# K's first head in one transfer and inside the loop, wo in six transfers, ten semaphores fewer

## The chip, the cores and the metric

The kernel runs on one core of one Trainium2 chip. The metric is the device time of one execution in microseconds. Before the change the median of three runs is 1363.03 us (1362.77 to 1363.04).

## What is computed

One decode step for one token: a layer norm, then attention over a cache of 16384 keys for 32 heads of 128, and beside it a gated feed-forward block; both are added to the input. All data is float32. Cut to what matters:

```python
# x (1,1,576); k_cache, v_cache (1,32,16384,128); wq (576,4096); wo (4096,576)
# w_gate, w_up (576,4608); w_down (4608,576)
xn = layernorm(x)
q = (xn @ wq).reshape(32, 128)
scores = einsum("hd,hkd->hk", q, k_cache) * 128 ** -0.5
a = einsum("hk,hkd->hd", softmax(scores), v_cache).reshape(4096) @ wo
g, u = xn @ w_gate, xn @ w_up
return x + a + (gelu(g) * u) @ w_down
```

The two caches are 537 MB of the 588 MB that are read.

## The kernel before

Every large operand passes through three buffers of 64 KB on each of 128 partitions: slot_a, slot_b and slot_v (sa, sb and sv in the code). One head of K or of V fills one of them whole (8.389 MB).

SP issues all large loads, in the order of its program, and each waits on SP until its buffer is free; so the order in the code is the order in the queue. First wq (sa) and the parts of wq, w_gate and w_up that go elsewhere, then w_gate's main part (sb), w_up's (sa), K's first head in two halves (sb, L380 to L382), K's second head (sa), V's first (sv). Then a loop (L387) alternates K and V: K's next head goes out when VectorE has given back a K slot (semaphore s_kf), V's next when TensorE has given back sv (s_vf). Behind the loop come 28 rows of w_down (sb), V's last head (sv), the rest of w_down (sa), and wo: its first 8 rows of each partition into sa, the other 24 into sb, over rows of w_down that VectorE has already summed.

VectorE computes the scores. For a head it multiplies the K slot by q (qs, broadcast), reduces over 128 elements, then takes the maximum over each partition (pm); TensorE transposes pm, and VectorE reduces that to nm. K's first head is done in front of the loop in two parts of 64 rows (L427 to L433), then 15 turns of two heads each (L434), then the last head (L437). ScalarE turns the scores into exponentials (pe, L450) and makes the next q; TensorE multiplies pe with V (L405). TensorE's loop runs 32 times, ScalarE's five loops together 32 times.

In front of that, x comes by three small loads that ScalarE issues: once as a row (xrow, for the layer norm) and once cut in two (x2, to be added at the end). The identity matrix ident is made by GpSimd; VectorE reduces it to small selection matrices (par, same, quarter, sel_p, sel_r, sel_l).

Behind the loops VectorE sums 28 rows of w_down, each times its element of h (L467 to L469), and 20 pieces of its last half row; TensorE takes the rest of w_down and the 32 rows of wo from the slots. wo's last twelve rows go in quarters to four PSUM banks (pg, pqs, po, pc), its very last row comes in two half rows; four copies and one DMA write the output.

Class Order records for each written region which semaphore value says that it is done, and sets the waits from that. A plain `load` makes a semaphore of its own (d0, d1, ...). `take(engine, s, n)` waits for n and subtracts it again.

Of the kernel before, what the change touches and what calls it, by code (L numbers as in the profile page):

```python
# [10 lines left out]
ALU = mybir.AluOpType  # L11
AX = mybir.AxisListType

P = 128
H, SK, DH = 32, 16384, 128
D, DF = 576, 4608
R = SK // P
SUB = 64
DJ = 4
DM = P * DJ  # L20
SCALE = DH**-0.5
# [1 line left out]
HALF = D // 2  # L23
# [3 lines left out]
WD_T = DF // P  # L27
# [1 line left out]
FB = (11 * WD_T, 11 * WD_T, 10 * WD_T)  # L29
WO_T = HD // P  # L30
WD_A = 28
WO_PIECES = (8, 12, 4, 4, 2, 1, 1)
WO_A = 8
WO_Q = 12
QUART = D // 4
FEW, EACH, RUN = 5, 4, 6
MANY, GROUP = FEW * EACH, EACH * RUN + 1
LEFT = P - FEW * EACH * RUN
# [5 lines left out]
class Order:  # L44
# [3 lines left out]

    def __init__(self, tc):
        self.tc, self.nc = tc, tc.nc  # L50
        self.sem = {e: tc.alloc_semaphore(f"s_{e}") for e in self.ENGINES[1:]}
        self.count = dict.fromkeys(self.sem, 0)
        self.seen = {e: {} for e in self.ENGINES}
        self.log = {}
# [36 lines left out]
    def op(self, eng, emit, out, *ins, also=(), signal=None, quiet=False):  # L91
        reads, writes = [a for a in ins if a is not None], [out, *also]
        need = self.needs(eng, reads, writes)
        for sem, value in need[:-1]:
            getattr(self.nc, eng).wait_ge(sem, value)
        i = emit(getattr(self.nc, eng))
        if need:
            i._wait_ge(*need[-1])
        value = self.count[eng] + 1
        if quiet:  # L100
            pass
        elif signal is None:
            self.count[eng] = value
            i.then_inc(self.sem[eng], 1)
        else:
            i.then_inc(signal, 1)
        self.note(eng, self.sem[eng], value, reads, writes)

    def dma(self, dst, src, sem, value=16, eng="sync", out=False):
        need = self.needs(eng, [src] if out else [], [] if out else [dst])  # L110
# [49 lines left out]
def decode(tc, x, k_cache, v_cache, wq, wo, wg, wu, wd, out, slots, s_ends):  # L160
# [5 lines left out]
    def sem():  # L166
        return tc.alloc_semaphore(f"d{next(names)}")
# [50 lines left out]
    def dve(name, out, *ins, **kw):  # L218
        o.op("vector", lambda e: getattr(e, name)(out, *ins, **kw), out, *[a for a in ins if isinstance(a, bass.AP)],  # L219
             *[a for a in kw.values() if isinstance(a, bass.AP)])  # L220
# [4 lines left out]

    spent = []

    def load(dst, src, again=False, **kw):
        if again and spent:
            o.dma(dst, src, spent.pop(0), value=32, **kw)  # L230
        else:
            s = sem()
            o.dma(dst, src, s, **kw)
            if kw.get("eng") != "scalar":
                spent.append(s)
        return dst

    ROW3 = 3 * DF
# [1 line left out]
    qt = load(sb[:, ROW3 : ROW3 + QS], wtail["q"])  # L240
    row3, tails, at = {}, {}, 0
    for n in "gu":
        row3[n] = load(sv[:, at : at + DF], wmain[n][:, ROW3:])
        tails[n] = load(sv[:, at + DF : at + DF + DF // 2], wtail[n])
        at += DF + DF // 2

    xrow = sv[:1, ROW3 + FG : ROW3 + FG + D]
    load(xrow, xf, eng="scalar")
    o.op("gpsimd", lambda e: e.memset(x2, 0.0), x2)
    s_x = sem()  # L250
    for i in range(2):
        o.dma(x2[32 * i : 32 * i + 1, :], xf[:, i * HALF : (i + 1) * HALF], s_x, value=32, eng="scalar")
    o.op("gpsimd", lambda e: e.memset(ident, 0.0), ident)
    o.op("gpsimd", lambda e: e.affine_select(out=ident, in_=ident, compare_op=ALU.not_equal, fill=1.0, base=0,
                                             pattern=[[-1, P]], channel_multiplier=1), ident, ident)
    o.op("vector", lambda e: e.memset(ones, 1.0), ones)
    o.op("vector", lambda e: e.memset(eps_t, EPS), eps_t)
    s_ap, s_vp, s_pa, s_v, s_pt, s_vf, s_kf, s_qf, s_qd, s_d, s_a = (tc.alloc_semaphore(f"h{n}") for n in range(11))
    s_k = [tc.alloc_semaphore(f"k{n}") for n in range(2)]
    for bank, s in ((PO, s_pa), (pc, None), (pq, None)):  # L260
        o.op("vector", lambda e, bank=bank: e.memset(bank, 0.0), bank, signal=s)
# [91 lines left out]
            i = nc.tensor.matmul(dst, lhs, rhs, start=start, stop=stop)  # L353
        i.then_inc(s, 1)

    def take(e, s, n=1):
        e.wait_ge(s, n).then_inc(s, -n)  # L357

    def head(h):
        return bass.ds(h, 1)  # L360
# [13 lines left out]
    def load_k(h, dst, s):  # L374
        nc.sync.dma_start(dst, kv[:, head(h), :].rearrange("p h f -> p (h f)")).then_inc(s_k[s], 16)

    def load_v(h):
        nc.sync.dma_start(sv, vv[:, head(h), :].rearrange("p h f -> p (h f)")).then_inc(s_v, 16)

    parts = [(sb[:, i * SUB * DH : (i + 1) * SUB * DH], S[:, i * SUB : (i + 1) * SUB]) for i in range(R // SUB)]  # L380
    for i, (dst, _) in enumerate(parts):
        load(dst, kv[:, 0, i * SUB * DH : (i + 1) * SUB * DH])  # L382
    o.wait("sync", [], [sa])
    load_k(1, sa, 1)
    o.wait("sync", [], [sv])
# [1 line left out]
    with nc.sync.Fori(0, (H - 2) // 2) as i:  # L387
        for s, dst in ((0, sb), (1, sa)):
            take(nc.sync, s_kf)
            load_k(i * 2 + (2 + s), dst, s)  # L390
            take(nc.sync, s_vf)
            load_v(i * 2 + (1 + s))

    with nc.Fori(0, H, engines=OrderedEngineSet([KIND["tensor"]]), head_slot={KIND["tensor"]: 0}):
        take(nc.tensor, s_ap)
# [12 lines left out]

    def highest(sc):
        nc.vector.reduce_max(pm, sc, axis=AX.X).then_inc(s_vp, 1)  # L410
        take(nc.vector, s_pt)
        nc.vector.tensor_reduce(nm[:1], pt[:1, :P], axis=AX.X, op=ALU.max, negate=True).then_inc(s_vp, 1)  # L412

    def scores_of(kt, s):
        sc = S[:, s * R : s * R + R]
        blk = kt.rearrange("p (n d) -> p n d", d=DH)
        take(nc.vector, s_k[s], 16)
        take(nc.vector, s_qd)
        nc.vector.tensor_mul(blk, blk, qs.unsqueeze(1).to_broadcast([P, R, DH])).then_inc(s_d, 1)  # L419
        nc.vector.wait_ge(s_d, 1).then_inc(s_qf, 1)  # L420
        nc.vector.tensor_reduce(sc, blk, axis=AX.X, op=ALU.add).then_inc(s_d, 1)  # L421
        nc.vector.wait_ge(s_d, 2).then_inc(s_kf, 1)
        take(nc.vector, s_d, 2)
        highest(sc)

    take(nc.vector, s_qd)
    for src, sc in parts:  # L427
        blk = src.rearrange("p (n d) -> p n d", d=DH)
        dve("tensor_mul", blk, blk, qs.unsqueeze(1).to_broadcast([P, SUB, DH]))
        dve("tensor_reduce", sc, blk, axis=AX.X, op=ALU.add)  # L430
    nc.vector.wait_ge(o.sem["vector"], o.count["vector"]).then_inc(s_kf, 1)
    nc.vector.nop().then_inc(s_qf, 1)
    highest(S[:, :R])  # L433
    with nc.vector.Fori(0, (H - 2) // 2):  # L434
        scores_of(sa, 1)
        scores_of(sb, 0)
    scores_of(sa, 1)  # L437

    for h0, n in ((0, 6), (6, 8), (14, 8), (22, 8), (30, 2)):
        row, lo = divmod(min(h0 + 2, H - 1), H // 4)  # L440
        with nc.scalar.Fori(0, n) as i:
            take(nc.scalar, s_pa)
            nc.scalar.activation(z, PO, AF.Copy).then_inc(s_ap, 1)  # L443
            take(nc.scalar, s_pa)
            take(nc.scalar, s_qf)
            nc.scalar.activation(qs, pq[:, :DH], AF.Copy).then_inc(s_qd, 1)
            take(nc.scalar, s_pa)
            nc.scalar.activation(nb, pb[:, :1], AF.Copy, scale=SCALE).then_inc(s_a, 1)  # L448
            take(nc.scalar, s_a)
            nc.scalar.activation(pe, S[:, bass.ds(i % 2 * R, R)], AF.Exp, bias=nb, scale=SCALE, accum_out=lsum[:, bass.ds(i + h0, 1)]).then_inc(s_ap, 1)  # L450
            take(nc.scalar, s_pa)
            nc.scalar.activation(oall[:, bass.ds(i + h0, 1)], pc[:, :1], AF.Copy)
            src = q_part(min(h0 + 2, H - 1)) if n == 2 else qb[32 * row : 32 * row + 1, bass.ds(i * DH + lo * DH, DH)]
            nc.scalar.activation(qcur, src, AF.Copy).then_inc(s_ap, 1)

    def load_rows(t, at, src, lo, n, cols=((0, D),)):
        for a, b in cols:
            if b - a == D:
                load(t[:, at * D : (at + n) * D], src[:, lo * D : (lo + n) * D], again=True)
            else:  # L460
                load(t[:, at * D + a : at * D + b], src[:, lo * D + a : lo * D + b], again=True)
        return [t[:, (at + j) * D : (at + j + 1) * D] for j in range(n)]

    take(nc.sync, s_kf)
# [6 lines left out]
    load_v(H - 1)  # L471
    take(nc.sync, s_kf)
    n = (WD_T - WD_A) * D - HALF
    load(sa[:, :n], wdv[:, WD_A * D : WD_T * D - HALF], again=True)
    wd_rows = [sa[:, j * D : (j + 1) * D] for j in range(WD_T - WD_A)]
    few = sa[AT : AT + MANY, n : n + (RUN + 1) * HALF]
    s_few, src = sem(), wdv[:, WD_T * D - HALF :]
    by_q = src[: FEW * GROUP].rearrange("(q t) f -> q t f", q=FEW)
    o.dma(few[:, : RUN * HALF], by_q[:, : GROUP - 1, :], s_few, value=48)
    o.dma(few[:FEW, RUN * HALF :], by_q[:, GROUP - 1, :], s_few, value=48)  # L480
    o.dma(few[FEW:LEFT, RUN * HALF :], src[FEW * GROUP :], s_few, value=48)
    few_sum = few[:, :HALF]
    dve("tensor_scalar", few_sum, few_sum, few_h[many, :1], None, op0=ALU.mult)
    for r in range(1, RUN + 1):
# [104 lines left out]
```

## Time and profile before

| what | us |
|---|---|
| median of three runs | 1363.03 |
| lowest and highest | 1362.77, 1363.04 |
| the profiled execution | 1362.84 |
| its span in the trace | 1361.1 |

| engine | busy us | share of the span |
|---|---|---|
| PE (TensorE matmul) | 445.6 | 33% |
| DVE (VectorE) | 1163.2 | 85% |
| ACT (ScalarE) | 68.6 | 5% |
| POOL (GpSimd) | 1.0 | 0% |

The span is the time between the first and the last event of the execution in the trace; times of rows count from its start. DMA engines do not stand in this table: the profile gives their mean busy share by slice, with the GB/s that they moved. SPq and ACTq are the sequencers of SP and ScalarE, which issue DMAs. "To landing" is the time from an issue to the arrival of its last byte.

### The profile page before, as it was taken

How to read it: one execution, taken by the hardware profiler on the slowest of the kernel's cores; microseconds unless marked ns; L12 is line 12 of the kernel's file. 1: busy time of each engine (PE TensorE's matmuls, PEld its weight loads, DVE VectorE, ACT ScalarE, POOL GpSimd, SP SyncE). 2: the span in 40 equal slices, each digit the busy share in tenths (PEclk: the TensorE clock that was granted, in tenths of full speed). 3: DMA queues.
4: the chain of work that ended last, by engine and by line, in shares of the span. 5: the costliest groups of instructions: out<-in, count | busy, mean ns of one | idle time of the engine just before them, and what ended most of it. 6: DMA issues, size and time to landing. Idle time of an engine off the chain costs nothing. (4 is left out here: it accounts for less than half of the span.)

```text
span 1361.1 us, 7835 instructions
## 1 busy us (share of the span) xinstructions
PE 445.6 (33%) x3032; PEld 162.0 (12%) x3032; DVE 1163.2 (85%) x208; ACT 68.6 (5%) x238; POOL 1.0 (0%) x7
## 2 busy tenths in 40 slices
PE   2431233323322333323223333233223333332236
PEld 1110111101111111101111111011111111011012
DVE  1069999999888888898888888998888889988883
ACT  0000000000000000000000000000000000000000
POOL 0000000000000000000000000000000000000000
PEclk9775666666556666666556666655566666655668
DMA  9999999999999999999999999999999999999998
GB/s 403 445 424 431 443 441 435 431 431 431 435 431 433 431 431 443 441 435 431 431 431 435 431 433 431 431 443 439 435 433 431 431 435 431 433 431 431 442 442 354
DMA packets 12106, 587.69 MB, mean 432 GB/s; under 512 B 1345, under 2 KB 1731, under 8 KB 1989
## 3 DMA queue, kind: packets, MB, share of 16 engines
q1 hardware_dynamic: 12093, 587.60, 99.7%
q8 instruction: 5, 0.08, 0.0%
q10 hardware_dynamic: 8, 0.01, 0.0%
HBM read 587.60 MB, written 0.00 MB: 432 GB/s over the span
## 5 line engine op out<-in xcount | busy, mean ns | idle before, releaser
L353 PE MATMUL po<-slot_v,pe 128*4 128x512 f32 x2048 | 291.5, 733 | 578.4 <-PEq L357 578.4
L419 DVE TENSOR_TENSOR slot_a<-slot_a,qs 128x16384 f32<-128x16384 f32 x16 | 275.6, 17226 | 34.9 <-DVEq L357 34.8
L419 DVE TENSOR_TENSOR slot_b<-slot_b,qs 128x16384 f32<-128x16384 f32 x15 | 258.4, 17226 | 32.3 <-DVEq L357 32.2
L421 DVE TENSOR_REDUCE scores<-slot_a 128x128 f32<-128x16384 f32 x16 | 275.5, 17220 | 2.3
L421 DVE TENSOR_REDUCE scores<-slot_b 128x128 f32<-128x16384 f32 x15 | 258.3, 17220 | 2.2
L353 PEld LDWEIGHTS po<-slot_v,pe 128*4 128x4 f32 x2048 | 56.4, 98 | 786.5 <-issue 786.5
L398 PE MATMUL pg<-ident,pm 128*1 128x128 f32 x32 | 11.9, 372 | 239.9 <-PEq L357 239.9
L443 ACT ACTIVATE z<-po 128x512 f32<-128x512 f32 x32 | 19.1, 597 | 827.8 <-ACTq L357 827.8
L353 PE MATMUL pc<-same,z 128*128 128x1 f32 x256 | 59.8, 355 | 0.0
L353 PEld LDWEIGHTS pc<-same,z 128*128 128x128 f32 x256 | 57.1, 328 | 0.5
L219 DVE TENSOR_TENSOR slot_v<-pg,same 128x396 f32<-128x396 f32 (+1 forms) x6 | 3.3, 558 | 52.2 <-PE pg L216 52.0
L398 PEld LDWEIGHTS pg<-ident,pm 128*1 128x1 f32 x32 | 2.5, 79 | 245.2 <-issue 245.2
L412 DVE TENSOR_REDUCE nm<-pg 1x1 f32<-1x128 f32 x32 | 8.9, 278 | 21.5 <-DVEq L357 21.5
L353 PE MATMUL pg<-nm,ones 1*128 1x1 f32 x64 | 17.7, 343 | 18.5 <-PEq L357 18.5
L219 DVE SCALAR_TENSOR_TENSOR slot_b<-slot_b,hT 128x576 f32<-128x576 f32 x27 | 22.1, 819 | 0.9
L353 PE MATMUL pqs<-qcur,ones 1*128 1x128 f32 x64 | 14.8, 312 | 21.9 <-PEq L357 20.7
L353 PEld LDWEIGHTS pg<-nm,ones 1*128 1x128 f32 x64 | 15.9, 308 | 27.8 <-issue 27.8
L448 ACT ACTIVATE nb<-pg 128x1 f32<-128x1 f32 x32 | 5.5, 172 | 243.1 <-ACTq L357 243.1
L219 DVE TENSOR_REDUCE scores<-slot_b 128x64 f32<-128x8192 f32 x2 | 17.4, 8686 | 0.1
L219 DVE TENSOR_TENSOR slot_b<-slot_b,qs 128x8192 f32<-128x8192 f32 x2 | 17.4, 8688 | 0.0
L410 DVE TENSOR_REDUCE pm<-scores 128x1 f32<-128x128 f32 x32 | 9.2, 286 | 8.2 <-DVEq L357 7.9
L353 PEld LDWEIGHTS pqs<-qcur,ones 1*128 1x128 f32 x64 | 9.6, 187 | 49.9 <-issue 49.9
(109 smaller groups left out, 158.2 us busy)
## 6 DMA issues: line engine op xcount, KB each, us to landing
slot_b<-in_A_k_cache_dram SPq DMA_DIRECT2D x2, 4096.0 KB, 24.1
slot_b<-in_B_w_down_dram SPq DMA_DIRECT2D x1, 8064.0 KB, 42.0
slot_b<-in_B_w_gate_dram SPq DMA_DIRECT2D x1, 6912.0 KB, 55.1
slot_a<-in_B_w_up_dram SPq DMA_DIRECT2D x1, 6912.0 KB, 37.9
slot_b<-in_A_wo_dram SPq DMA_DIRECT2D x1, 3456.0 KB, 27.6
slot_v<-in_B_w_gate_dram SPq DMA_DIRECT2D x1, 2304.0 KB, 28.7
slot_v<-in_B_w_up_dram SPq DMA_DIRECT2D x1, 2304.0 KB, 37.1
slot_a<-in_A_wo_dram SPq DMA_DIRECT2D x1, 2304.0 KB, 31.1
```

The lines of the kernel that those rows point to most:

```text
L219: o.op("vector", lambda e: getattr(e, name)(out, *ins, **kw), out, *[a for a in ins if isinstance(a, bass.AP)], *[a for a in kw.values() i ...
L353: i = nc.tensor.matmul(dst, lhs, rhs, start=start, stop=stop)
L398: nc.tensor.transpose(pt[:1, :P], pm, ident).then_inc(s_pt, 1)
L410: nc.vector.reduce_max(pm, sc, axis=AX.X).then_inc(s_vp, 1)
L412: nc.vector.tensor_reduce(nm[:1], pt[:1, :P], axis=AX.X, op=ALU.max, negate=True).then_inc(s_vp, 1)
L419: nc.vector.tensor_mul(blk, blk, qs.unsqueeze(1).to_broadcast([P, R, DH])).then_inc(s_d, 1)
L421: nc.vector.tensor_reduce(sc, blk, axis=AX.X, op=ALU.add).then_inc(s_d, 1)
L443: nc.scalar.activation(z, PO, AF.Copy).then_inc(s_ap, 1)
L448: nc.scalar.activation(nb, pb[:, :1], AF.Copy, scale=SCALE).then_inc(s_a, 1)
```

## The change

K's first head is loaded whole with load_k, as every other head is, and VectorE's loop runs 16 turns from the first head to the last; the code in front of it and behind it goes. In the SP queue one transfer of 8.389 MB stands where two halves stood:

```order
L113 DMA slot_a<-in_B_w_up_dram 128x13824 [waits s_tensor]
L113 DMA slot_b<-in_A_k_cache_dram 128x8192 [waits d7,s_tensor]
L113 DMA slot_b<-in_A_k_cache_dram 128x8192 [waits d0,s_tensor]
L375 DMA slot_a<-in_A_k_cache_dram 128x16384 [waits s_tensor,d8]
L378 DMA slot_v<-in_A_v_cache_dram 128x16384 [waits d4,d3,s_vector,d2,d1]
```

That was SP before its loop in the kernel before; and this is the same place in the changed kernel:

```order
L115 DMA slot_a<-in_B_w_up_dram 128x13824 [waits s_tensor]
L378 DMA slot_b<-in_A_k_cache_dram 128x16384 [waits s_tensor,d4,d0]
L378 DMA slot_a<-in_A_k_cache_dram 128x16384 [waits s_tensor,d5]
L381 DMA slot_v<-in_A_v_cache_dram 128x16384 [waits s_vector,d2,d1]
L389 UNCONDITIONAL_BRANCH
```

The whole head waits for w_gate's main part (now d4) and for q's tail (d0), for which the two halves waited one each. On VectorE, from the last step of the feed-forward block to the loop, before (h8 says that qs is there, h4 that TensorE has transposed pm):

```order
L219 TENSOR_TENSOR slot_b<-slot_b,qs 128x8192 [waits h8,d7,d9]
L219 TENSOR_REDUCE scores<-slot_b 128x64 [waits s_vector]
L219 TENSOR_TENSOR slot_b<-slot_b,qs 128x8192 [waits d10]
L219 TENSOR_REDUCE scores<-slot_b 128x64 [waits s_vector]
L410 TENSOR_REDUCE pm<-scores 128x1 [waits s_vector]
L412 TENSOR_REDUCE nm<-pg 1x1 [waits h4]
L434 UNCONDITIONAL_BRANCH
L419 TENSOR_TENSOR slot_a<-slot_a,qs 128x16384 [waits k1,h8]
```

and now (h7 says that qs is there, k0 and k1 that the K slots are filled):

```order
L430 UNCONDITIONAL_BRANCH
L423 TENSOR_TENSOR slot_b<-slot_b,qs 128x16384 [waits k0,h7]
L425 TENSOR_REDUCE scores<-slot_b 128x128 [waits s_vector]
L414 TENSOR_REDUCE pm<-scores 128x1 [waits s_vector]
L416 TENSOR_REDUCE nm<-pg 1x1 [waits s_tensor]
L423 TENSOR_TENSOR slot_a<-slot_a,qs 128x16384 [waits k1,h7]
```

The multiply starts with the whole head in its slot, and the loop begins with slot_b. In the same loops three semaphores give way to the engines' own, with their count at that point as the base (a_base, pt_base, d_base).

wo comes in pieces of 16, 8, 4, 3 and 1 rows (the last in two halves) instead of 8, 12, 4, 4, 2, 1 and 1; 16 rows go to slot_a instead of 8. SP's last transfers before:

```order
L113 DMA slot_a<-in_A_wo_dram 128x4608
L113 DMA slot_b<-in_A_wo_dram 128x6912 [waits d0,s_vector]
L113 DMA slot_b<-in_A_wo_dram 128x2304 [waits s_vector] x2
L113 DMA slot_b<-in_A_wo_dram 128x1152 [waits s_vector]
L113 DMA slot_b<-in_A_wo_dram 128x576 [waits s_vector]
L113 DMA slot_b<-in_A_wo_dram 128x288 [waits s_vector]
L113 DMA slot_b<-in_A_wo_dram 128x288
```

and now:

```order
L115 DMA slot_a<-in_A_wo_dram 128x9216
L115 DMA slot_b<-in_A_wo_dram 128x4608 [waits k0,s_vector]
L115 DMA slot_b<-in_A_wo_dram 128x2304 [waits s_vector]
L115 DMA slot_b<-in_A_wo_dram 128x1728 [waits s_vector]
L115 DMA slot_b<-in_A_wo_dram 128x288 [waits s_vector]
L115 DMA slot_b<-in_A_wo_dram 128x288
```

Rows 28, 29 and 30 of wo now arrive as one piece. The code's own semaphores go from 31 to 21: the two parts of w_gate and of w_up that go to sv share one each, the three loads of x and the identity share one (value 49: three times 16, and 1 from GpSimd), and later loads take over semaphores that are done with. x2 and ident are cleared by VectorE instead of GpSimd. The rest of the diff, cut to what these words name:

```diff
-WO_PIECES = (8, 12, 4, 4, 2, 1, 1)
-WO_A = 8
+WO_PIECES = (16, 8, 4, 3, 1)
+WO_A = 16
...
-        self.sem = {e: tc.alloc_semaphore(f"s_{e}") for e in self.ENGINES[1:]}
+        self.sem = {e: tc.alloc_semaphore(f"s_{e}") for e in ("scalar", "vector", "tensor")}
...
+    def step(self, eng):
+        return self.sem[eng], self.count[eng]
...
-        row3[n] = load(sv[:, at : at + DF], wmain[n][:, ROW3:])
-        tails[n] = load(sv[:, at + DF : at + DF + DF // 2], wtail[n])
+        s = sem()
+        spent.append((s, 48))
+        row3[n] = load(sv[:, at : at + DF], wmain[n][:, ROW3:], s, 32)
+        tails[n] = load(sv[:, at + DF : at + DF + DF // 2], wtail[n], s, 32)
...
-    load(xrow, xf, eng="scalar")
-    o.op("gpsimd", lambda e: e.memset(x2, 0.0), x2)
+    o.op("vector", lambda e: e.memset(x2, 0.0), x2)
     s_x = sem()
+    o.dma(xrow, xf, s_x, value=49, eng="scalar")
...
-    parts = [(sb[:, i * SUB * DH : (i + 1) * SUB * DH], S[:, i * SUB : (i + 1) * SUB]) for i in range(R // SUB)]
-    for i, (dst, _) in enumerate(parts):
-        load(dst, kv[:, 0, i * SUB * DH : (i + 1) * SUB * DH])
+    o.wait("sync", [], [sb])
+    load_k(0, sb, 0)
...
-    take(nc.vector, s_qd)
-    for src, sc in parts:
-        blk = src.rearrange("p (n d) -> p n d", d=DH)
-        dve("tensor_mul", blk, blk, qs.unsqueeze(1).to_broadcast([P, SUB, DH]))
-        dve("tensor_reduce", sc, blk, axis=AX.X, op=ALU.add)
-    nc.vector.wait_ge(o.sem["vector"], o.count["vector"]).then_inc(s_kf, 1)
-    nc.vector.nop().then_inc(s_qf, 1)
-    highest(S[:, :R])
-    with nc.vector.Fori(0, (H - 2) // 2):
+    with nc.vector.Fori(0, H // 2):
+        scores_of(sb, 0)
         scores_of(sa, 1)
-        scores_of(sb, 0)
-    scores_of(sa, 1)
```

## Rows read from the trace of the kernel before

**Rows 1.** The page: DMA busy tenths and GB/s in 40 slices, total bytes.

```profile
DMA  9999999999999999999999999999999999999998
GB/s 403 445 424 431 443 441 435 431 431 431 435 431 433 431 431 443 441 435 431 431 431 435 431 433 431 431 443 439 435 433 431 431 435 431 433 431 431 442 442 354
DMA packets 12106, 587.69 MB, mean 432 GB/s; under 512 B 1345, under 2 KB 1731, under 8 KB 1989
```

**Rows 2.** Busy time by stretch; the first line names the columns.

```profile
core 0: us, PE busy (x) PEld busy (x) DVE busy (x) ACT busy (x) POOL busy (x), PEclk, DMA share, GB/s
0.00:22.90 22.90, 0.00 (x1) 0.03 (x1) 4.77 (x18) 1.58 (x2) 0.97 (x7) 1.00 0.92 386
500.00:1000.00 500.00, 159.14 (x995) 55.86 (x994) 454.85 (x51) 25.07 (x88) 0.00 (x0) 0.61 1.00 434
1350.00:1356.66 6.66, 5.64 (x120) 2.79 (x120) 0.90 (x2) 0.00 (x0) 0.00 (x0) 1.00 0.98 401
```

**Rows 3.** The chain that ended last: start us, us, what.

```profile
1330.92 25.74 DMA slot_b<-in_A_wo_dram
```

**Rows 4.** SP's timeline: start us, us, engine, line, operation; transfers' issues.

```profile
0.74 0.45 SPq L133 DMA_DIRECT2D slot_a<-in_A_wq_dram  x1
...
64.87 0.33 SPq L113 DMA_DIRECT2D slot_b<-in_A_k_cache_dram  x1
...
66.84 0.33 SPq L113 DMA_DIRECT2D slot_b<-in_A_k_cache_dram  x1
...
86.22 0.33 SPq L378 DMA_DIRECT2D slot_v<-in_A_v_cache_dram  x1
122.72 0.35 SPq L375 DMA_DIRECT2D slot_b<-in_A_k_cache_dram  x1
```

**Rows 5.** DMA issues at 64.87, 66.84 and 86.22: KB, us to landing.

```profile
slot_b<-in_A_k_cache_dram SPq DMA_DIRECT2D x1, 4096.0 KB, 20.3
...
slot_b<-in_A_k_cache_dram SPq DMA_DIRECT2D x1, 4096.0 KB, 28.0
...
slot_v<-in_A_v_cache_dram SPq DMA_DIRECT2D x1, 47.2
```

**Rows 6.** Timeline around K's first two heads, VectorE and ScalarE.

```profile
122.62 0.29 DVE L410 TENSOR_REDUCE pm<-scores 128x1 f32<-128x128 f32 x1 [0.26 <-DVE scores L219]
123.92 17.23 DVE L419 TENSOR_TENSOR slot_a<-slot_a,qs 128x16384 f32<-128x16384 f32 x1
125.44 0.19 ACT L450 ACTIVATION_READ_ACCUMULATOR pe<-scores,nb  x1
...
158.77 0.29 DVE L410 TENSOR_REDUCE pm<-scores 128x1 f32<-128x128 f32 x1 [0.26 <-DVEq L357]
```

**Rows 7.** Timeline of the start, VectorE and TensorE.

```profile
3.47 0.23 DVE L219 TENSOR_REDUCE par<-ident 128x2 f32<-128x128 f32 x1
...
4.54 0.23 DVE L219 COPY sel_l<-ident 128x5 f32<-128x5 f32 x2
...
12.43 0.21 DVE L219 COPY slot_v<-slot_v 1x128 f32<-1x128 f32 x1
...
22.90 1.30 PE L216 MATMUL pc<-ones,slot_v 1*128 1x1 f32 x5 [22.90 <-PEq L239]
```

**Rows 8.** VectorE's timeline: the first step of the sum over w_down.

```profile
1311.59 0.52 DVE L219 TENSOR_SCALAR slot_b<-slot_b,hT 128x576 f32<-128x576 f32 x1 [1.99 <-DMA slot_b<-in_B_w_down_dram]
```

**Rows 9.** Timeline of the end: TensorE on wo's last rows, the output's issue.

```profile
1357.40 0.28 PE L216 MATMUL pg<-slot_b,oT 128*1 128x144 f32 x1
...
1357.52 0.28 PE L216 MATMUL pg<-slot_b,oT 128*1 128x144 f32 x1
...
1357.75 0.28 PE L216 MATMUL pg<-slot_b,oT 128*1 128x144 f32 x1
...
1358.13 0.28 PE L216 MATMUL po<-slot_b,oT 128*1 128x144 f32 x1
...
1358.93 0.24 ACTq L556 DMA_DIRECT2D out_dram<-row  x1
```

More of the change, by code (lines that the diff above doesn't have):

```diff
@@ L17 @@
 R = SK // P
-SUB = 64
 DJ = 4
@@ L226, in decode, with load @@
     spent = []
[L228 to L231, printed above, removed]
+    def load(dst, src, s=None, value=16):
+        if s is None:
             s = sem()
-            o.dma(dst, src, s, **kw)
-            if kw.get("eng") != "scalar":
-                spent.append(s)
+            spent.append((s, 32))
+        o.dma(dst, src, s, value=value)
         return dst
@@ L242, in decode @@
     for n in "gu":
-        row3[n] = load(sv[:, at : at + DF], wmain[n][:, ROW3:])
-        tails[n] = load(sv[:, at + DF : at + DF + DF // 2], wtail[n])
+        s = sem()
+        spent.append((s, 48))
+        row3[n] = load(sv[:, at : at + DF], wmain[n][:, ROW3:], s, 32)
+        tails[n] = load(sv[:, at + DF : at + DF + DF // 2], wtail[n], s, 32)
         at += DF + DF // 2
     xrow = sv[:1, ROW3 + FG : ROW3 + FG + D]
-    load(xrow, xf, eng="scalar")
-    o.op("gpsimd", lambda e: e.memset(x2, 0.0), x2)
+    o.op("vector", lambda e: e.memset(x2, 0.0), x2)
     s_x = sem()
+    o.dma(xrow, xf, s_x, value=49, eng="scalar")
     for i in range(2):
[L252 to L255, printed above, removed]
+        o.dma(x2[32 * i : 32 * i + 1, :], xf[:, i * HALF : (i + 1) * HALF], s_x, value=49, eng="scalar")
+    o.op("vector", lambda e: e.memset(ident, 0.0), ident)
+    o.wait("gpsimd", [ident], [ident])
+    nc.gpsimd.affine_select(out=ident, in_=ident, compare_op=ALU.not_equal, fill=1.0, base=0,
+                            pattern=[[-1, P]], channel_multiplier=1).then_inc(s_x, 1)
+    o.note("gpsimd", s_x, 49, [], [ident])
     o.op("vector", lambda e: e.memset(ones, 1.0), ones)
     o.op("vector", lambda e: e.memset(eps_t, EPS), eps_t)
-    s_ap, s_vp, s_pa, s_v, s_pt, s_vf, s_kf, s_qf, s_qd, s_d, s_a = (tc.alloc_semaphore(f"h{n}") for n in range(11))
+    s_ap, s_vp, s_pa, s_v, s_vf, s_kf, s_qf, s_qd = (tc.alloc_semaphore(f"h{n}") for n in range(8))
     s_k = [tc.alloc_semaphore(f"k{n}") for n in range(2)]
@@ L354, in chain, with take @@
         i.then_inc(s, 1)
-    def take(e, s, n=1):
-        e.wait_ge(s, n).then_inc(s, -n)
+    def take(e, s, n=1, base=0):
+        e.wait_ge(s, base + n).then_inc(s, -n)
     def head(h):
@@ L392, in decode @@
             load_v(i * 2 + (1 + s))
+    (s_a, a_base), (s_pt, pt_base), (s_d, d_base) = (o.step(e) for e in ("scalar", "tensor", "vector"))
     with nc.Fori(0, H, engines=OrderedEngineSet([KIND["tensor"]]), head_slot={KIND["tensor"]: 0}):
@@ L410, in highest @@
         nc.vector.reduce_max(pm, sc, axis=AX.X).then_inc(s_vp, 1)
-        take(nc.vector, s_pt)
+        take(nc.vector, s_pt, base=pt_base)
         nc.vector.tensor_reduce(nm[:1], pt[:1, :P], axis=AX.X, op=ALU.max, negate=True).then_inc(s_vp, 1)
@@ L419, in scores_of @@
         nc.vector.tensor_mul(blk, blk, qs.unsqueeze(1).to_broadcast([P, R, DH])).then_inc(s_d, 1)
-        nc.vector.wait_ge(s_d, 1).then_inc(s_qf, 1)
+        nc.vector.wait_ge(s_d, d_base + 1).then_inc(s_qf, 1)
         nc.vector.tensor_reduce(sc, blk, axis=AX.X, op=ALU.add).then_inc(s_d, 1)
-        nc.vector.wait_ge(s_d, 2).then_inc(s_kf, 1)
-        take(nc.vector, s_d, 2)
+        nc.vector.wait_ge(s_d, d_base + 2).then_inc(s_kf, 1)
+        take(nc.vector, s_d, 2, d_base)
         highest(sc)
-    take(nc.vector, s_qd)
-    for src, sc in parts:
-        blk = src.rearrange("p (n d) -> p n d", d=DH)
-        dve("tensor_mul", blk, blk, qs.unsqueeze(1).to_broadcast([P, SUB, DH]))
-        dve("tensor_reduce", sc, blk, axis=AX.X, op=ALU.add)
-    nc.vector.wait_ge(o.sem["vector"], o.count["vector"]).then_inc(s_kf, 1)
-    nc.vector.nop().then_inc(s_qf, 1)
-    highest(S[:, :R])
-    with nc.vector.Fori(0, (H - 2) // 2):
+    with nc.vector.Fori(0, H // 2):
+        scores_of(sb, 0)
         scores_of(sa, 1)
-        scores_of(sb, 0)
-    scores_of(sa, 1)
     for h0, n in ((0, 6), (6, 8), (14, 8), (22, 8), (30, 2)):
@@ L448, in decode @@
             nc.scalar.activation(nb, pb[:, :1], AF.Copy, scale=SCALE).then_inc(s_a, 1)
-            take(nc.scalar, s_a)
+            take(nc.scalar, s_a, base=a_base)
             nc.scalar.activation(pe, S[:, bass.ds(i % 2 * R, R)], AF.Exp, bias=nb, scale=SCALE, accum_out=lsum[:, bass.ds(i + h0, 1)]).then_inc(s_ap, 1)
@@ L454, in decode @@
             nc.scalar.activation(qcur, src, AF.Copy).then_inc(s_ap, 1)
+    spare = [(s_k[0], 16), (s_k[1], 16), *spent]
     def load_rows(t, at, src, lo, n, cols=((0, D),)):
         for a, b in cols:
[L458 to L461, printed above, removed]
+            w = D * (n - 1) + b
+            load(t[:, at * D + a : at * D + w], src[:, lo * D + a : lo * D + w], *(spare.pop(0) if spare else ()))
         return [t[:, (at + j) * D : (at + j + 1) * D] for j in range(n)]
@@ L473, in decode @@
     n = (WD_T - WD_A) * D - HALF
-    load(sa[:, :n], wdv[:, WD_A * D : WD_T * D - HALF], again=True)
+    load(sa[:, :n], wdv[:, WD_A * D : WD_T * D - HALF], *spare.pop(0))
     wd_rows = [sa[:, j * D : (j + 1) * D] for j in range(WD_T - WD_A)]
     few = sa[AT : AT + MANY, n : n + (RUN + 1) * HALF]
-    s_few, src = sem(), wdv[:, WD_T * D - HALF :]
+    src = wdv[:, WD_T * D - HALF :]
     by_q = src[: FEW * GROUP].rearrange("(q t) f -> q t f", q=FEW)
-    o.dma(few[:, : RUN * HALF], by_q[:, : GROUP - 1, :], s_few, value=48)
-    o.dma(few[:FEW, RUN * HALF :], by_q[:, GROUP - 1, :], s_few, value=48)
-    o.dma(few[FEW:LEFT, RUN * HALF :], src[FEW * GROUP :], s_few, value=48)
+    o.dma(few[:, : RUN * HALF], by_q[:, : GROUP - 1, :], s_x, value=97)
+    o.dma(few[:FEW, RUN * HALF :], by_q[:, GROUP - 1, :], s_x, value=97)
+    o.dma(few[FEW:LEFT, RUN * HALF :], src[FEW * GROUP :], s_x, value=97)
     few_sum = few[:, :HALF]
```

## The prediction

> **What bounds the kernel now.** I read the page's strip of 40 slices first. The line of the DMA engines stands at 9 tenths or more in every slice but the last, and the line under it at 424 to 445 GB/s from the second slice to the thirty-ninth [rows 1]. The table by stretches says the same with a number: 434 GB/s and a DMA share of 1.00 from 500 to 1000 us, while VectorE works 455 of those 500 us and TensorE 159 [rows 2]. So the time is that of 587.69 MB through sixteen engines that never rest: 587.69 MB at 434 GB/s is 1354.1 us, and what is left of the 1361.1 us span is the start before the first byte and the tail after the last one.
>
> The second view is the chain that ended last, and here it misleads. It goes through VectorE's sum over w_down to a transfer of wo that took 25.74 us [rows 3]. That transfer is two rows of wo, 0.59 MB or 1.4 us at 434 GB/s; the other 24 us it stood in the queue, behind V's last head and what followed. A faster VectorE would only have made it stand longer. I therefore treat an edit as free unless it makes the queue run dry, changes the bytes or how fast they go, or changes what stands before the first byte or behind the last.
>
> **The change part by part.**
>
> *The start.* x2 and ident are cleared by VectorE instead of GpSimd, and three small loads and the identity now share one semaphore, so the reduces over ident wait for x. They ran from 3.47 to 4.77 us, before x had come [rows 7]; behind the loads they put 1.3 us on the way to the normalised row, and I allow 0.8 us more for the second and third load of x, which are issued after the first. The normalised row, ready at 12.64 us, is then ready by about 14.7. TensorE starts on it at 22.90 us, when wq is there [rows 7]. Cover 10.3 us, use 2.1: nothing. Without that cover it would cost at most 2.1 us. SP, which issues the big loads, does not stand behind any of it.
>
> *K's first head whole.* Its two halves were issued at 64.87 and 66.84 us and landed 20.3 and 28.0 us later, at 85.2 and 94.84 [rows 4, 5]. The whole one waits for what the second half waited for, so it is issued near 66.84. The first half's 9.66 us of data, landed at 85.2, did not flow before 75.5; the queue had other work until then, 8.7 us after the new issue, and the whole head lands near 94.84 as before: no byte is later. VectorE is the one that loses. It began on the first half while the second was under way, and was at the maximum (pm) by 122.62 [rows 6]. Now it begins at 94.84. From the start of a whole head's multiply to its pm takes 158.77 - 123.92 = 34.85 us [rows 6], so pm comes at 129.7, 7.1 us later. SP stood waiting for that with K's third head: its issue followed pm by 0.10 us (122.72 [rows 4]), now at 129.8.
>
> Is the queue empty then? V's first head was issued at 86.22 and landed 47.2 us later, at 133.42 [rows 4, 5]. The third K head was in the queue 10.7 us before that; now it is 3.6 us before. What a transfer needs between issue and flow, the start bounds: wq is issued at 0.74 [rows 4], and the first 22.90 us moved 386 GB/s [rows 2], 8.84 MB, which at 434 GB/s is 20.4 us of flow, hence a start at 2.5 and 1.8 us of lead (an estimate from these rows). 3.6 is more than 1.8, so the cost is nothing; the other end, that 10.7 us were needed, is 7.1 us. I take zero, since the 1.8 us are of the same queue. Behind it the lead grows again, for VectorE is busy 455 us of 500 [rows 2] and gains on the queue with every head.
>
> The other stage that waits for pm is the product with V. The exponentials were ready at 125.63, 3.0 us behind pm [rows 6]; at 132.7 they are still ahead of V's landing at 133.42. Were they a microsecond late, V's second head would be issued that much later; it stands in the queue behind K's third, whose 8.389 MB take 19.3 us, so that is nothing either.
>
> *The loop's end.* K's last head is inside VectorE's loop now, so the loop exit lies before the w_down sum. VectorE stood 1.99 us for that transfer at 1311.59 [rows 8]; an exit within that is hidden, and a later sum only shortens the stand of wo in the queue. Half of wo now goes to slot_a and waits for no sum, the rest for 16 rows of it at most instead of 24. Nothing.
>
> *Fewer transfers.* One K half and two pieces of wo are gone, the bytes are the same. What a transfer costs in a full queue, the two K halves show: they landed 94.84 - 85.17 = 9.67 us apart, and 4.194 MB at 434 GB/s is 9.66 us [rows 2, 5]. The last two pieces of 147 KB were taken up 0.38 us apart (1357.75 and 1358.13 [rows 9]) against 0.34 us at 434. So 0.01 to 0.04 us each, 0.1 us for three. The largest gain: all that the last stretch loses, 6.66 us at 401 instead of 434 GB/s [rows 2], 0.5 us. I take -0.1.
>
> The Trainium skill speaks for more. Its page "DMA: Bandwidth & Descriptors" (Anatomy of one DMA) gives each DMA a fixed cost of about 2.0 us beside its bytes, and its rules tell authors to merge transfers. By that the three would give 6 us. The rows above bear out another reading of the same page, that most of the fixed cost is the receipt at the end, which a queue that is already moving the next bytes does not wait for.
>
> *The last piece on TensorE.* Before, single row 30 came at 1357.40 and was through two passes 0.12 us apart, ahead of the half row at 1357.75 [rows 9]. Now rows 28 to 30 land together at that moment: three rows, six passes, 0.73 us, to 1358.13, and then two passes for each half row. The last pass starts at 1358.38 to 1358.50 instead of 1358.25. The two copies and the output DMA at 1358.93 [rows 9] shift with it: +0.13 to +0.25, I take +0.2.
>
> *Ten semaphores fewer,* 21 of the code's own 31 left. The trace has no row for what one costs. From the end of the last DMA issue (1359.17 [rows 9]) to the span's end are 1.93 us, and 1.74 us of the profiled 1362.84 lie outside the span; were all of it spent on semaphores in proportion, ten would give back 1.2 us. The other end is zero, and the nearest rows (a landing takes most of it) speak for that end. I take -0.1.
>
> **Sum:** 0 + 0 + 0 - 0.1 + 0.2 - 0.1 = 0.0 on 1362.84 us. That execution is 0.19 us under the median of 1363.03, so 1363.0.
>
> **The rivals.**
>
> *The queue runs dry at K's third head (slower).* Place: after V's first head, at 133.4 us. It decides as soon as the queue needs more than 3.6 us from issue to flow; each microsecond above is one at the end, since nothing later has slack to pay it back. If it needed the whole 10.7 us of before: 7.1 us, 1370.1 us. For it: the sixteen engines need not end V together, and those that are ahead want the next bytes sooner than the landing shows. Against it: the 1.8 us of the start. A loss of 1 us is thinkable and would give 1364.0, one above 2.7 needs a lead of 6.3 us. 6 in 100 for a loss that is over 0.2%, 6 for one under it.
>
> *Each transfer has a price on the path (faster).* If every transfer paid the 1.8 us that wq paid at the start, three fewer would give 5.4 us: 1357.6 us. The halves' 0.01 us speaks against it. 3 in 100. (The 2.0 us of the Trainium skill's page on DMA would make it 1357.0.)
>
> *Semaphores and merged pieces give their bounds.* -0.5 - 1.2 + 0.2 from above: 1361.5 us, still within 0.2%. 10 in 100.
>
> *The loop exit holds VectorE's sum, and wo with it (slower).* The wo pieces would come in after the queue had drained; the two-row piece stood 24 us [rows 3], so a stall of 27 us would be needed to cost 3: 1366.0 us, 1 in 100.
>
> **How the numbers follow.** Forecast 74 in 100, semaphores and pieces 10, small gap 6, large gap 6, price per transfer 3, loop exit 1. The predicted time is the forecast's, 1363.0. The range takes in the semaphore bound at the low end, 1361.4, and a gap of 1.6 us at the high end, 1364.6; beyond it lie the large gap, the price per transfer and the exit, 10 in 100, and a few more of what I did not think of. Faster by over 0.2% (2.7 us, about what a measurement of this kernel can tell from no change) 0.05, slower by as much 0.07, within it 0.88.
>
> **What would show it.** Right: the third K head's issue near 129.8 us, its landing still near 152.7; pm near 129.7; GB/s still 434 in the middle; the output DMA issued at 1358.9 to 1359.2. Wrong: a dip in the DMA share around 131 to 134 us, a third K head that lands 1 us or more later, a pm later than 130.5, or a TensorE that starts after 22.90.

## The result: 2.06 us slower

| kernel | median us | lowest, highest | runs |
|---|---|---|---|
| before | 1362.85 | 1362.70, 1363.04 | 22 |
| changed | 1364.91 | 1363.63, 1366.09 | 22 |

The ratio is 1.0016 (95% interval 1.0010 to 1.0021). The forecast was 1363.0 in a range up to 1364.6; the median lies 0.31 us above that range. The change costs time, about three quarters of what the forecast called measurable, and it does a second thing: the runs, which lay within 0.34 us of each other, now lie within 2.46 us.

The profiled execution of the changed kernel took 1364.10 us, 1.26 more than the one of before, with a span of 1362.3 us; it is one of the quicker of its 22. From the page of the changed kernel, the answer to [rows 1]:

```profile
DMA  9999999999999999999999999999999999999998
GB/s 403 445 424 429 431 435 439 441 433 431 433 435 431 433 431 437 441 437 433 431 435 433 433 431 431 443 437 435 433 431 437 431 433 431 435 439 441 432 430 355
DMA packets 11674, 587.69 MB, mean 431 GB/s; under 512 B 1297, under 2 KB 1683, under 8 KB 1813
```

The bytes are the same, and a slice of 34 us shows no hole. The hole is smaller than a slice, so it has to be looked for where the change moved an issue. The timeline of SP (start us, us, operation), then the issues at 86.03 and 129.93 with their us to landing, as in [rows 4, 5]:

```profile
86.03 0.33 SPq L381 DMA_DIRECT2D slot_v<-in_A_v_cache_dram  x1
129.93 0.35 SPq L378 DMA_DIRECT2D slot_b<-in_A_k_cache_dram  x1
142.47 0.34 SPq L381 DMA_DIRECT2D slot_v<-in_A_v_cache_dram  x1
```

```profile
slot_v<-in_A_v_cache_dram SPq DMA_DIRECT2D x1, 47.3
...
slot_b<-in_A_k_cache_dram SPq DMA_DIRECT2D x1, 24.0
```

V's first head landed at 86.03 + 47.3 = 133.33, so K's third head was in the queue 3.4 us before that. It landed at 153.93, 20.6 us behind V, where 8.389 MB take 19.3. Before, the issue at 122.72 ([rows 4]) landed at 152.7:

```profile
slot_b<-in_A_k_cache_dram SPq DMA_DIRECT2D x1, 30.0
```

Those 1.2 us are still there at the end. Of VectorE's timeline, the first step of the w_down sum ([rows 8]), and of ScalarE's, the output's issue ([rows 9]):

```profile
1312.81 0.52 DVE L221 TENSOR_SCALAR slot_b<-slot_b,hT 128x576 f32<-128x576 f32 x1 [1.95 <-DMA slot_b<-in_B_w_down_dram]
```

```profile
1360.25 0.24 ACTq L551 DMA_DIRECT2D out_dram<-row  x1
```

1312.81 - 1311.59 = 1.22 us, and 1360.25 - 1358.93 = 1.32 us. Some 1150 microseconds of full queue took nothing of it back and added next to nothing: what the queue loses at 130 us is lost.

### The profile page after: what moved, and what is told of

It is laid out like the page before. It is cut to its first block, busy times and chain, and to the rows that moved or that the text cites. A ratio compares the mean times of both kernels' runs of the same rounds, so it can differ in the third digit from the quotient of the medians.

```text
span 1362.3 us, 7830 instructions
## 1 busy us (share of the span) xinstructions
PE 447.7 (33%) x3032; PEld 162.0 (12%) x3032; DVE 1163.4 (85%) x208; ACT 68.6 (5%) x238; POOL 0.5 (0%) x5
## 5 line engine op out<-in xcount | busy, mean ns | idle before, releaser
L423 DVE TENSOR_TENSOR slot_b<-slot_b,qs 128x16384 f32<-128x16384 f32 x16 | 275.6, 17226 | 36.6 <-DVEq L360 36.6
L425 DVE TENSOR_REDUCE scores<-slot_b 128x128 f32<-128x16384 f32 x16 | 275.5, 17220 | 2.3
L356 PE MATMUL pqs<-qcur,ones 1*128 1x128 f32 x64 | 14.8, 312 | 21.8 <-PEq L360 20.6
L218 PE MATMUL pg<-slot_b,z 128*32 128x396 f32 (+1 forms) x72 | 8.9, 671 | 17.1 <-DMA slot_b<-in_B_w_gate_dram 17.1
```

Source lines behind the costliest of these rows:

```text
L218: o.op("tensor", lambda e: e.matmul(outp, lhsT, rhs, start=start, stop=stop), outp, lhsT, rhs, signal=signal, quiet=quiet)
```

## Experiments

The theory, "short lead": K's third head reaches the queue 3.4 us ahead of the end of V's first, and that is too late for sixteen engines to go on without a break. Rivals: the new pieces of wo ("tail"), or the small edits (one semaphore for x and ident, memsets on VectorE, fewer semaphores, the loop). Medians below stand beside runs of the kernel before on the same chip: 1362.99 us for the first four kernels, 1362.91 for the delays of 4.0, 5.2 and 9.0 us and the old pieces of wo, 1362.93 for the delays of 11.0 and 14.0 us and the new pieces.

**Undo the whole head alone.** The changed kernel with two halves in front of the loop:

```diff
-    load_k(0, sb, 0)
...
+    for i, (dst, _) in enumerate(parts):
+        load(dst, kv[:, 0, i * SUB * DH : (i + 1) * SUB * DH])
...
-    with nc.vector.Fori(0, H // 2):
...
+    for src, sc in parts:
...
+    with nc.vector.Fori(0, (H - 2) // 2):
+        scores_of(sa, 1)
         scores_of(sb, 0)
-        scores_of(sa, 1)
+    scores_of(sa, 1)
```

> The changed kernel with K's first head in two halves in front of VectorE's loop again; wo in six transfers, the shared semaphores and the memsets on VectorE stay. Theory short lead (K's third head is issued only 3.4 us before V's first head has landed, and some DMA engines run dry there; that costs most of the 2.06 us): the lead is back at 10 us or more, time 1363.0 to 1363.2, the 0.25 us of the last piece stay, and the runs lie within 0.4 us of each other again. Rival tail (the pieces of wo cost it): 1364.5 to 1365. Rival small edits (x and ident behind one semaphore, the loop, the semaphores): 1364.5 to 1365.

Measured: 1363.05 us (1362.81 to 1363.32). The loss is gone and the spread with it. What is left of the change, six transfers of wo, nine fewer semaphores (the halves take one back) and the shared waits, costs 0.06 us, which these runs can't tell from nothing.

**Undo the pieces of wo as well**, so that only the semaphores (eight fewer than before) and the memsets are left:

```diff
-WO_PIECES = (16, 8, 4, 3, 1)
-WO_A = 16
+WO_PIECES = (8, 12, 4, 4, 2, 1, 1)
+WO_A = 8
```

> The changed kernel with K's first head in halves and with wo in the eight old transfers; only the shared semaphores and the memsets on VectorE are left of the change. Theory short lead: 1362.6 to 1362.9, the time of the kernel before or some tenths less for the semaphores. Rival tail: the same. Rival small edits: 1364 to 1365.

Measured: 1362.92 us (1362.79 to 1363.10), 0.07 under the kernel before, again nothing that can be told from zero. The rival "small edits" falls.

**Do the whole head alone.** The kernel before, with the opposite of the first edit:

```diff
...
-    for i, (dst, _) in enumerate(parts):
-        load(dst, kv[:, 0, i * SUB * DH : (i + 1) * SUB * DH])
+    o.wait("sync", [], [sb])
+    load_k(0, sb, 0)
...
-    with nc.vector.Fori(0, (H - 2) // 2):
+    with nc.vector.Fori(0, H // 2):
+        scores_of(sb, 0)
         scores_of(sa, 1)
-        scores_of(sb, 0)
-    scores_of(sa, 1)
```

> The kernel before with K's first head loaded whole and done in VectorE's loop, nothing else (the two semaphores of the halves fall away). Theory short lead: 1364.3 to 1365, with runs spread over 2 us as in the changed kernel, and K's third head lands 20 us or more behind V's first instead of 19.3. Rivals tail and small edits: 1362.7 to 1363.0, narrow.

The two semaphores of the halves fall away, but two of the last loads take new ones, so there are 31 as before. Measured: 1364.82 us (1363.72 to 1365.29): 1.83 us and a spread of 1.6. Its issues on SP's timeline, V's first and K's third head, and their us to landing:

```profile
87.24 0.33 SPq L378 DMA_DIRECT2D slot_v<-in_A_v_cache_dram  x1
...
130.08 0.35 SPq L375 DMA_DIRECT2D slot_b<-in_A_k_cache_dram  x1
```

```profile
slot_v<-in_A_v_cache_dram SPq DMA_DIRECT2D x1, 46.3
...
slot_b<-in_A_k_cache_dram SPq DMA_DIRECT2D x1, 24.5
```

V landed at 133.54, K's third head at 154.58, 21.0 us behind it. So the loss belongs to this part of the change.

**The late issue without the whole head.** The kernel before keeps its halves, but VectorE does one more reduce before it gives the slot back; pm is overwritten behind it:

```diff
+    dve("tensor_reduce", pm, sb[:, :6720], axis=AX.X, op=ALU.max)
     nc.vector.wait_ge(o.sem["vector"], o.count["vector"]).then_inc(s_kf, 1)
```

> The kernel before, halves and all, with one more reduce on VectorE (7.1 us, its result is overwritten) between the last reduce of K's first head and the signal that gives its slot back. So K's third head is issued as late as in the changed kernel, with nothing else of the change. Theory short lead: 1364.3 to 1365 with a spread of 2 us. If the whole transfer itself or the loop is to blame and not the late issue: 1362.7 to 1363.0.

Measured: 1365.08 us (1364.13 to 1365.46), 2.09 us, just above what was expected, with a spread of 1.3. Not the size of the transfer nor the loop, but the lateness of the next issue makes the loss. The rest of the series changes only the width of that reduce (3776, 4910, 8496, 10384 and 13216 elements for 4.0, 5.2, 9.0, 11.0 and 14.0 us).

> The kernel before with the extra reduce on VectorE cut to 4.0 us, so that K's third head is issued near 127.6 us, some 6 us ahead of V's landing. Theory short lead with a threshold: the engines' own spread (about 2 us) and the 1.8 us from issue to flow fit into 6 us, so 1362.9 to 1363.2, narrow. If every microsecond of lead counts, from 10.7 downwards: about 1364.

Measured: 1362.89 us (1362.73 to 1363.42): nothing.

> The same with a reduce of 5.2 us: K's third head is issued some 4.7 us ahead of V's landing. Theory short lead with a threshold: at its edge, 1363.0 to 1363.8. If every microsecond counts: about 1364.4.

Measured: 1363.24 us (1362.80 to 1364.44): +0.33, from runs without any loss to one with 1.5 us. The profiled one is of the former, with its issue at 127.74, no later than in the kernel above (127.86), though its reduce is 1.2 us longer: from execution to execution VectorE comes to the halves earlier or later, here by 1.3 us (V's first head was issued at 86.07 here and at 87.38 there). So the edge lies a little under 5.6 us.

> The same with a reduce of 9.0 us: lead of about 1 us. Theory short lead: below the threshold each microsecond of lead is one of time, so 2 us above the kernel with 7.1 us (1365.08): 1366.6 to 1367.4, and now narrow again, since all engines stand. If the loss came from something else than the lead (a fixed cost of a queue that restarts): 1365 to 1365.5.

Measured: 1365.80 us (1365.26 to 1366.56): +2.89, less than the 3.7 or more that I had expected, and with a spread of 1.3 us not narrow either.

> The kernel before with an extra reduce of 11.0 us in K's first head: K's third head is issued about 1 us after V's first has landed. Theory short lead: the queue is empty now, so from the kernel with 9.0 us (1365.8, lead 1.4 us) on each microsecond of delay is one of time: 1367.4 to 1368.4. Rival, a restart costs a fixed 2 to 3 us however late it comes: 1365.8 to 1366.3.

Measured: 1367.38 us (1366.51 to 1368.43): +4.45, just under the lower edge of what was expected, with a spread of 1.9.

> The same with 14.0 us, 3.0 us more than the kernel with 11.0. Theory short lead: 3.0 us above that one, 1370.4 to 1371.4. Rival, a fixed cost of the restart: 1366.

Measured: 1371.14 us (1370.91 to 1371.33): +8.21, narrow. Its issue came 137.78 - 134.06 = 3.7 us after that of the kernel with 11.0 us in the profiled executions, and its time is 3.8 us longer: with an empty queue each microsecond is one. A fixed price of a restart, the rival there, falls. Its own rows:

```profile
137.78 0.35 SPq L375 DMA_DIRECT2D slot_b<-in_A_k_cache_dram  x1
```

```profile
slot_b<-in_A_k_cache_dram SPq DMA_DIRECT2D x1, 21.9
```

Put in order by the lead (V's landing less the issue of K's third head, both of the profiled execution). The median is that of all runs; the last column has the one execution that the lead was read from, against the profiled execution of the kernel before. "Old pieces" is the changed kernel with the old pieces of wo, further below:

| kernel | lead us | K's third head behind V's first, us | median against before, us | profiled execution against before's, us |
|---|---|---|---|---|
| before | 10.7 | 19.3 | 0 | 0 |
| only semaphores left | 9.8 | 19.3 | -0.07 | +0.04 |
| 4.0 us delay | 5.6 | 19.3 | -0.02 | +0.08 |
| 5.2 us delay | 5.6 | 19.4 | +0.33 | -0.04 |
| whole head alone | 3.5 | 21.0 | +1.83 | +2.10 |
| changed | 3.4 | 20.6 | +2.06 | +1.26 |
| old pieces | 3.4 | 21.2 | +2.12 | +2.87 |
| 7.1 us delay | 2.7 | 21.7 | +2.09 | +2.38 |
| 9.0 us delay | 1.4 | 20.4 | +2.89 | +3.19 |
| 11.0 us delay | -0.7 | 22.8 | +4.45 | +4.66 |
| 14.0 us delay | -4.3 | 26.2 | +8.21 | +8.24 |

The lead says whether there is a loss, but not to the microsecond how much: three executions with 3.4 or 3.5 us lost 1.3 to 2.9.

The view that shows it without any landing is the table by stretches, read over the 9 us around the hand-over, 128 to 137 us (columns as in [rows 2], the last is GB/s). In this order the kernel before, the changed one, the whole head alone, the 9.0 and the 14.0 us delay:

```profile
128.00:137.00 9.00, 3.42 (x20) 0.64 (x24) 9.00 (x1) 0.00 (x0) 0.00 (x0) 0.50 1.04 451
```

```profile
128.00:137.00 9.00, 6.13 (x31) 3.01 (x35) 8.07 (x4) 1.06 (x5) 0.00 (x0) 0.52 1.05 437
```

```profile
128.00:137.00 9.00, 6.00 (x27) 2.91 (x31) 8.07 (x4) 1.06 (x5) 0.00 (x0) 0.50 0.95 379
```

```profile
128.00:137.00 9.00, 3.96 (x19) 2.62 (x23) 8.01 (x4) 1.33 (x6) 0.00 (x0) 0.50 0.92 371
```

```profile
128.00:137.00 9.00, 0.00 (x0) 0.00 (x0) 9.00 (x1) 0.00 (x0) 0.00 (x0) 0.50 0.30 131
```

451, 437, 379, 371, 131 GB/s. The table counts a packet where it starts, so one packet of 64 KB is 7 GB/s of such a stretch, and a share can pass 1. The other kernels with a lead of 5.6 us or more have 451 or 466 in this stretch, but other stretches of 9 us of the kernel before go from 386 to 459. The last three rows therefore show the hole; the 437 of the changed kernel would be no proof by itself, and its share of 1.05 shows nothing.

The single records of the kept traces show it there too. They hold the start and the duration of every packet, and for every transfer sixteen completions, the last of which is the landing; no view prints them one by one.

- *V's first head does not end at once.* In the kernel before thirteen of its completions come from 131.66 to 132.28 us and the other three from 133.11 to 133.45; in the changed kernel from 131.55 to 132.05 and from 133.19 to 133.33. Counted to the first completion, the lead of the changed kernel is 1.6 us and not 3.4.
- *An issue does not flow at once.* In the kernel with 14.0 us, where the queue was empty, the issue at 137.78 started its first packet at 138.77 and its sixteenth at 139.77.
- *The loss has two parts.* Down to a lead of 5.6 us sixteen packets are in flight without a break, and each packet of 64 KB takes 2.42 us. With a shorter lead some of the sixteen places stand empty, and the packets that follow take longer, up to 3.4 us in the changed kernel. From 126 to 150 us, as a mean of the sixteen:

| kernel | lead to V's first completion, us | places empty, us | longer packets, us | mean completion of K's third head, late by us |
|---|---|---|---|---|
| before | 8.9 | 0 | 0 | 0 |
| 4.0 us delay | 3.8 | 0.00 | 0.00 | 0.02 |
| changed | 1.6 | 0.20 | 0.38 | 0.58 |
| whole head alone | 1.5 | 0.25 | 0.81 | 1.08 |
| 9.0 us delay | -0.3 | 1.51 | 0.61 | 2.21 |
| 14.0 us delay | -6.1 | 7.15 | 0.66 | 7.85 |

The two parts add up to the lateness within 0.1 us in each row, so hardly anything else was lost there.

**The pieces of wo alone**, from both sides. On the kernel before the first edit, on the changed one its opposite:

```diff
-WO_PIECES = (8, 12, 4, 4, 2, 1, 1)
-WO_A = 8
+WO_PIECES = (16, 8, 4, 3, 1)
+WO_A = 16
```

> The kernel before with wo in pieces of 16, 8, 4, 3 and 1 rows and nothing else. TensorE has three rows instead of one to do when the last but one piece lands: plus 0.1 to 0.25 us, 1363.0 to 1363.2, narrow; the output DMA is issued 0.1 to 0.25 us later than at 1358.93. If the larger pieces help the queue more than that: 1362.5 to 1362.9.

Measured: 1363.14 us (1362.97 to 1363.24): +0.21. And the changed kernel with the old pieces:

> The changed kernel with wo in its eight old transfers. The pieces of wo were put at +0.2 for TensorE and -0.1 for the queue: so 0.1 to 0.25 us less than the changed kernel's 1364.9, with the same spread of 2 us. If the pieces had a larger part in the loss: 1363.5 to 1364.3.

Measured: 1365.03 us (1363.26 to 1365.71), 0.12 above the changed kernel instead of 0.1 to 0.25 below it, and well inside the spread of both: this side tells nothing. In the first of the two, ScalarE's timeline has the output's issue where the forecast put it:

```profile
1359.07 0.24 ACTq L556 DMA_DIRECT2D out_dram<-row  x1
```

1359.07 - 1358.93 = 0.14 us.

No run points to a version that beats the kernel before: the best of these, 1362.89 to 1363.05, are its equals.

## Why the prediction was wrong, step by step

**What bounds the kernel** held. What did not make the queue run dry cost 0.2 us at most, and what did came through undiminished, as the 1.2 us from 154 to 1360 us show.

**The start** held in its result and failed in its size. From the changed kernel's timeline, VectorE and TensorE, the answer to [rows 7]:

```profile
19.84 0.29 DVE L221 TENSOR_REDUCE par<-ident 128x2 f32<-128x128 f32 x1 [15.84 <-DMA x<-in_A_x_dram]
```

```profile
23.31 2.02 PE L218 MATMUL pc<-ones,slot_v 1*128 1x1 f32 x8 [23.31 <-DVE slot_v L221]
```

I had allowed 0.8 us for the second and third load of x; they could be used 9.6 us behind the first, 19.84 against 10.25, when VectorE began on the first load's row before:

```profile
10.25 0.81 DVE L219 BATCH_NORM_STATS2 small<-slot_v 1x6 f32<-1x288 f32 x2 [5.48 <-DMA slot_v<-in_A_x_dram]
```

The trace of the kernel before had it already: there the second and the third load completed at 15.11 and 19.99 us, but nothing waited for them. The whole cover of 10.3 us was used, and TensorE began 0.41 us late, which hurt nothing. K's first head was issued at 68.26 instead of near 66.84, but the start is not shown to be the reason: the second half was issued at 68.25 in the kernel with the 5.2 us delay, which has the old start. It landed at 94.8 all the same. The kernel with only the semaphores and memsets left shows no loss.

**When VectorE is done with K's first head** held to 0.2 us: the maximum was forecast at 129.7 and came at 129.85, from VectorE's timeline (compare [rows 6]):

```profile
95.00 17.23 DVE L423 TENSOR_TENSOR slot_b<-slot_b,qs 128x16384 f32<-128x16384 f32 x1 [7.51 <-DVEq L360]
...
129.85 0.29 DVE L414 TENSOR_REDUCE pm<-scores 128x1 f32<-128x128 f32 x1 [0.26 <-DVEq L360]
```

The issue was forecast at 129.8 and came at 129.93; the lead at 3.6, and was 3.4.

**"3.6 is more than 1.8, so the cost is nothing"** is the step that failed. The 1.8 us from issue to flow were about right: the empty queue of the 14.0 us kernel started its sixteen first packets 1.0 to 2.0 us after the issue. The 3.6 us were the wrong thing to hold against them, and a term was missing. First, the 3.6 us ran to V's landing, which is the last of sixteen completions. Thirteen of them came 1.6 to 2.1 us after the issue (131.55 to 132.05 against 129.93), so most of the queue had a lead of about the time to flow, with nothing to spare. The forecast named this as an argument for its rival and gave it no price. Second, the sum put nothing for what follows a late start: packets that take longer, 0.38 of the 0.58 us that K's third head was late in the mean. So 5.6 us to the landing (3.8 to the first completion) were enough, and 3.4 (1.6) cost 2.

From issue to landing the empty queue took 21.9 us, 2.6 more than the flow of 8.389 MB, and wq at the start was much the same: TensorE waited for it until about 22.90 ([rows 7]), 22.2 us after its issue, 2.8 more than the flow. Part of that surplus is first packets that take longer than 2.42 us, which a time to the start of flow leaves out.

**The rival "the queue runs dry"** was the case that came. It put the loss in the right place and said rightly that nothing later pays it back; its error was the slope. It let each microsecond under the threshold cost one, and called its small form 1364.0. The medians show nothing lost down to 5.6 us of lead, a rise to 2 us by 3.4, only 0.8 us more down to 1.4, and one for one when the queue is empty. A straight line back from the two late kernels, 8.21 - 4.3 = 3.9 us and 4.45 - 0.7 = 3.8 us less the lead, would give 0.5 us at 3.4; 2.06 were measured. The packet records say part of why: the longer packets do not shrink with the lead, but cost 0.4 to 1.0 us in every kernel with a loss. They also say why the end can be later than K's third head was. In the kernel with 9.0 us that head landed 1.2 us late, but its first completion came 2.4 us late (153.44 against 150.99), and the output was issued 3.2 us late, at 1362.11; a landing tells of the last completion alone. **What stays open** is why packets take longer after a short lead, why such kernels spread over 1.3 to 2.5 us, and where the rest of the loss comes from behind K's third head: in the kernel with 9.0 us the mean lateness grows from 2.2 us there to 3.0 at V's sixth head, and that was not followed up.

**Fewer transfers and the last piece** held: -0.1 and +0.2 forecast, +0.21 measured for both together on the kernel before, +0.13 between the first two experiments, each smaller than the spread of the runs. In the profiled executions the last half row of wo landed 0.18 us earlier with the new pieces (1357.91 against 1358.09) and the output was issued 0.14 us later. **Ten semaphores** were put at -0.1; -0.07 was measured for eight of them with the memsets in it, and either is nothing. **A price per transfer** of 1.8 or 2.0 us is refuted: two transfers of wo fewer bought no time, and the kernel with 1363.05 us has one transfer more than the changed kernel and is the quicker one. The 2.0 us, which the prediction took from the Trainium skill's page "DMA: Bandwidth & Descriptors" (Anatomy of one DMA), are given in that section for DMAs that GpSimd issues; the large transfers here are SP's.

**The chances:** 0.88 stood for "within 0.2%" (2.7 us), and 2.06 us is within it. That this came true is luck rather than merit: 84 of the 100 stood for no gap at all, and only 6 for a gap of this size. The range went wrong with the step above: its upper end held a gap of 1.6 us, and the gap with the tail came to 2.06.

## What to carry to other kernels

When a transfer bounds a kernel, an edit that delays some engine is free only while the next issue still comes early enough. Work out the lead of each moved issue before the transfer ahead of it ends, know that its first parts are done before it lands, and trust only leads that runs show to be enough (here 9.8 us before the landing and more; 5.6 were at the edge); a lead estimated from how fast a queue starts is not one of them. A load in two halves can be worth its second transfer for this alone: it lets the consumer begin early, and so gives its buffer back early.

## What the runs showed of the hardware

- A queue of 64 KB rows on sixteen engines ran on without loss in executions where the next 8.389 MB were issued 5.6 us ahead of the last landing; at 3.4 or 3.5 us the medians lost 1.8 to 2.1 us, and from an empty queue 3.9 us plus the lateness of the issue (8.21 us at 4.3 us late).
- A transfer of 8.389 MB in a full queue was not done at once: three of its sixteen completions came 0.8 to 1.8 us behind the other thirteen (V's first head, kernel before: 131.66 to 132.28, then 133.11 to 133.45).
- An issue into an empty queue started its first packets 1.0 to 2.0 us later (137.78; 138.77 to 139.77), and these took 2.4 to 3.4 us where a packet of a full queue took 2.42.
- A loss of that kind also shows as a spread. Undisturbed kernels lay within 0.3 to 0.7 us, those with a lead of 1 to 4 us within 1.3 to 2.5 us. A median that grows together with its spread is a hint to look for a hand-over at the edge.
- Three loads of 1 to 2 KB that ScalarE issued within a microsecond of each other, beside wq's 8.389 MB, did not land together: the first row could be used at 10.25 us, the others at 19.84. In the kernel before their three packets started at 7.41, 12.33 and 17.21 us, 4.9 us apart, which is twice the 2.42 us of a 64 KB packet.
